# A new hand-recorded issue order for TensorE in an attention and gated feed-forward kernel, with a corrected planner's clock

## The chip, the cores and the metric

The kernel runs on one core of a Trainium2 chip. The metric is the time of one execution on the device, in microseconds (us). TensorE does matrix products (a 128 x 128 array of rows and columns); VectorE, ScalarE and GpSimd work element by element; SyncE (SP) issues nearly all DMA transfers. Results of products land in PSUM, which has eight banks of 128 x 512 fp32.

## The reference

What is computed, cut to what matters. There are 2048 tokens of 512 features, 32 heads of 16, and a hidden layer of 1792.

```python
x = A_x
xn = layernorm(x)                                    # over the 512 features, eps 1e-5
q, k, v = split_heads(xn @ A_wqkv)                   # 32 heads of 16
p = softmax(einsum("bhqd,bhkd->bhqk", q, k) * 16 ** -0.5)
s = merge_heads(einsum("bhqk,bhkd->bhqd", p, v)) @ A_wo
h = silu(xn @ B_w1) * (xn @ B_w3)
g = silu(h @ B_w2)
return x + s * g
```

All of it is fp32. Most products are made with numbers split in a high and a low part, three products instead of one (`split3`, `three`).

## The kernel before, in words

A prologue of some 160 us normalises x, transposes it, makes q, k and v and stores them. Then one long stretch does attention and feed-forward at the same time, and a tail does the projection with `wo` and the final sum.

**Attention** goes in 32 phases (16 pairs of heads, two halves of 1024 queries each). Three kinds of TensorE work belong to it:

- *Maxima* (letter m or M): `max_unit` multiplies 128 queries with 512 keys of one head; VectorE takes the row maximum out of the bank (line 391). When a phase's 64 maxima are there, `max_rows` reduces them, ScalarE negates them, TensorE turns them (line 404, the steps called by r and R), and four small DMAs write them as two extra rows of the queries, so that the score product subtracts the maximum by itself.
- *Scores* (s or S): `scores` multiplies 128 keys with 512 queries of one head (line 626); ScalarE takes the exponential out of the bank into one of 23 buffers `pt` (line 629, `PTS`).
- *Values* (v or r): `values` multiplies four buffers of exponentials with the values, four products side by side in 32 columns each (line 639), and adds up in the bank `pv`. One such group of four is a value block; 16 blocks make a phase, 512 the whole. After a phase, `take_out` copies `pv` out and, in several steps some us apart (`LATER`, `SOON`), fetches the row sums, makes their reciprocal, spreads it by DMA through HBM into `rb`, multiplies on GpSimd and stores the result.

**Feed-forward** (f or F): `gate` makes the hidden layer and the gate in four blocks of 512 tokens (`ORDER` 3, 0, 1, 2). `Lanes.emit` (line 857) issues each product in two halves of 64 rows.

Maxima, scores and gate products use 64 of the array's 128 rows each. A small letter uses the lower half (lane 0), a capital the upper half (lane 1), so that two of them run side by side. Value blocks and output tiles (o: `projecting`, with line 195, 197 and 199 in `split3`; `finish` at lines 1034 and 1035) use all 128 rows.

TensorE takes its instructions in program order. That order is written out by hand in the string `ORDER_OF_ISSUE`, one letter a product: the loop at the end goes through it, and puts off a letter (`late`) whose conditions aren't met. The conditions come from the class `Model`, the kernel's own account of time at build time: `half`, `whole`, `block` move TensorE's two lanes on, `work` moves the other engines on, and `free_at`, `ready`, `made` and `there` say when a bank, a phase, a hidden tile or a transfer is there by that account. The same account decides when the side work is issued: weight loads and splits (`Weights`), output steps (`small`, the list `outs`), final loads (`tend`). On the chip only semaphores count; the account only fixes the order. Seven banks go round by `take`; `pv` has the eighth.

An instruction waits for semaphores of other engines, and of its own engine where a buffer is written again; a second wait is an instruction of its own (`EVENT_SEMAPHORE`).

Of the kernel before, what the change touches and what calls it, by code (L numbers as in the profile page):

```python
# [41 lines left out]

LATER = (16.0, 1.5, 9.0, 16.0, 5.0, 0.0)
# [7 lines left out]
    "MfMfMfMffSSfSffMffMfMfSfSfMfsFFfFfFsMffMFfsMmFfFsFFfFmmFFfMmvvSffMMfMffMfSfMfFfFfFsFmFsFfFfFsFmFsFfF"  # L51
    "fMfSfMfSffMsFFfmFmFsFFfmFmFsFfFmFMffFmSvvsMsMfMvfSfMMmsFfFFffFSfFfsMfFFsMfsFFfMsfFfFFmMmvSfSmFfFmmFf"
    "FSfmFSfFffSFfmSFfmFSfFfFsmMfFMmvvSmmMfFFfFsfFfFFfsFMffFMfsFfFfMMsfFfFMmvSmSmfFFfFfSfMffFsMsFfFMfSfFf"
    "mFSfmFmFmFFfmSvvsMSmmSvSmMmsFrsMsMFfFfMfSfFfMmvSmmFFfSffMFfsFMffSFfsFFmFffMfSfSfFmFsFmFsFFfsFmFsFFsm"
    "FfFMfMfMfvvMmSsfMfSvvsMSsfFmFfFFfFmfSFsmFfFsFmFSfFfMfFfMfMmSfvsMMfMsvSfMmsFFsFfFfsFmFsFFfSmFfmFSffFm"
    "FmSvmSSsMffMvsMfMfMmSvSfMsMmvsSsFmFmFFffFsFFfMsfFsFMffSfFmFmFSfSfMfvsMSfSmfMvSmmSrsFmSmSvmSSffMfSfFF"
    "fmFsFsFMffSFfMfsFFfmSfFfFsSsFMmvvMsMssMvMsfMfSFsFfFfmSFfFmsFMfFfSfmFFfSfMfFsMfFfsFSfmMvMsSfmMfSvvSmM"
    "fSsSfvfMfSSfSsvMfsMsFfFsFFfFmsFfFFmSfMfSfFfmFSfFfMfsSfFmFSffFmFSffFmFsFFmmFFmvsSMfMffMSfvsMsMsMvsMMs"
    "MfvSmmMvSfMfSffMfSFfMfsFMfFfsMfFsFMfFfsFMfsFMffFsFmFfFsFmFFmsFfFmFsFfFMfFfMmvSmmSMfvSsMmvrSmmSmSvsMM"
    "mFmmFvvFmFsmFSfFffSMffFSfMfsFFsMfFfsFmFFsfFsMfFSfMfFfsFMffSfSMfFffSmFsFFfSmvSmmMSmvvSmfFFffSmFfSSfFm"  # L60
    "FfFsmFFsfFmFsFmFFssFFfmFFsFfmFsFFmfSfSvmSSfMmvsMfMSfFsfFFfMsFfFssFMffFsMfFmFfFsFmFMmvvsMmSSmvvSfMfSs"
    "SfvrsMMssSvmFsFSffMsFFfmFFsfFMsFfSfMfSffFmSfFFmFmMfvSmSfmMvSfMffSfMfFsFmFFsFfmFSfmFFfsFfMfSmFfFFmMfM"
    "mvvmMSssFmFvSmsSMsvsMFfSffMsFfFsMFffMfMSffFsFMffFSfmFFmFmvsMmFmSvSmMffSfFfSfFmSfFsFSfmFfFsFmFfSFffFm"
    "MMfFmvvSfMsMsfFfFFfsFSfMffFFsfSMfFfsFsFMfFfmMvsMmFmFsFvsMMsSsvMsfFfSmFfSFfMfsFSfMfSfFfmFSffFsMfFmFmF"
    "mFvvSmmSmFrSfFmFfSfmFMfsFMffFsFFmfFSffMfFSmFffFSsvMsMssFFmvsMmMsSvvmSfFfFfMSfFfmSfSfFfMsFfFmSfFFsFmf"
    "MfFsMvvSmsMsMvsMfMMfFsfFFfSfMffFSffMFmfSFfmFmFsFfFmFmFvSfSmmFfFFfFsfMfMFsfFsFfMFsFffMsFsFfMMffFmSvmS"
    "mMsFsFvSmMmmSvSsmMvSfMfFsfMfFSffMMfsFFfsFfMFsfFFmSffMFsFmvsMmSvSmFfSfmFfSfFmFfSFfmFsFfFmSfFSfmFFsfFR"
    "vmSfMMsSfvSmsSSmvMsSffFMfSfFfsMfFFfmSFfFsMfsFfFMsFffMsFsFFfmMvsMmSSmvvmSSffSMffMvvSffMMmMffSvSmSsfFf"
    "FFfFsFsFmfFFmFfFsmFfSFmFfsFFmFmSfFffFSfMffSMfsFFfMffSfMFfsMvvsMsMfMvSmMsfMvSmMffSSfFffFMffMsFFfMfsFf"
    "FsFfMsFfFMsfFsFfMsFfFfMsFsFFfMfsFfSfFmFfFSmsFvvsSmSmMvvSmmSmSvvSmFffFmFFfSfMfFffMmFSffFfFfMmFSfFmfFr"  # L70
    "sFfMmFMffFsFfFfFFfMmsFsFfMFfvvMffSfSMfSffSmFfFFfmSFfFmsFFfsFmFFfsFmFsFmFsFFfFsmFFssFsFvmSSmSmvvSmsFs"
    "FsFmFvmSmSfFFfSffFMfSfSfFmFffMSfFfFmFsSfmMvvMsmFFsmFFsvsMsFsMsFvMsFffSMffFSfMfSffSMffFFsmFfFMfmSvSmS"
    "mSsvmFsSsMvMsmFmSsFvsMfSfMfFfSfFMsFffMsFfFfSmFfFfSFmmFfMRvsMmSvSsmFmFmMvvMfMssFFfFfSfMfSfFfSfMfMffFs"
    "FFsFmFfFfMfMffSfSfMfSfFfFmFsFmFsFfFmSfFsFmFfFFmSmvvsMsSmMvSfMsSfFfFmFfsFmFfSFfmFsFsFSfmFfFmFfMvSmMmM"
    "svvsMSffSSmvMsfMfSfMfSfSffSFmFffSFmfFsFmFsFfFSmfFFmfFmFmMsvvSmFfFmsSFffFmSfFFfmFsFFfMsmFFfmFfSrsMMsf"
    "MvsMMfsMMfvSfMmSmvsMmFsFFfSffFsFMfsFFfmSfFMfSffMFfsFmFFfMmvsSmMfMvvMssMfMFfFfFfFssFFfMfFsfFFsMffMSff"
    "FfSFmFffSfMfSFfmFFsfFmFsFmFFsFfFsmFFmmSvvSmMsmSvsMSsMfSfvmSfSSmfSvmSMfMsvsMfMsFFfsFFfMsFfsFFmSffFsFM"
    "fSfmFmFfFMfSffMvSfMsfMsFfFFfMfsFMffFsMfFSfFfmFSfmFmFmFFfMsvvsMmSmSvSmsSfFFmFfFfmSFfSfmFfFsFmFFfsFmFf"
    "SSfMfRvMsmMsSvmSMmfMSfvsMfMMsvfSfMfSfMSffMSffMvvMfSfSmmFFfFfFsFfFsFmfFFsFmfSfSFmFfFsMfsFfFsMFfMfsFSf"
    "fFMfSffFmSFfMfmFSfvsSmMMsvvSmmFmSmFvSmsFsSvMsfFsFfMfFsFMsfFfMfFSffMFfsMfFfSsFMffFfMsFFsFfMffSFfMsfFM"  # L80
    "fsFFmFfMmvSsMsmFvmMsSMmvvSmmSmSvvSmsMmSvrSmFmfFFmsFfFSfFmFfSffMSfMfFfsFMfsFfFMfsFfFfMMsfFFfFsmFFmFfF"
    "fMffSSsvmSMfsMvvMsSmfFFffFsFmFFsFfmFsFFmfSFsfFmFFsfFmFsFfFMsFmFfSfMfFfmSvvsMmSSmvSmSffSmFFffFmFsFmFm"
    "FFsFfSffFFmSffMMfMfFfSsvvMsMsMmvvSfMfsFfSfFfFMfsMSfFfsFfFmFsFFfsFMffFSsmFvmSfSSfmFFffFfSmFfSfSfMfFFs"
    "sFmFfFsFMfFfmFmMvvsMmSmFrSmSmvSmSffSmFfFfFmSfFsFFmsFfFMsfFfFmFSffMMsvsMsMsMvsMMfMfSmvvMffSfSFffMfFfS"
    "fMFsSffMfFFsmFsFfFmFsFFmmFvvSmFfFfFmmSFffFSmfFFmSffFFsFmFsFfMffMSfMfvsMMmMsvsMmSvsFMsfFfMSfFfSfmFSff"
    "FSmfFFsmFFffSmSFfFmmFvSmMssMvsMMsMfvsMMsvsMfMMffSfFFfsFfFfMMsFfFfSfFmmFsFfFfFFmmSvSmfSFmFfSffFMsfFFs"
    "sFMfFfsFmFFffSmFfFSmrmSMfmSSfvSmMssMvsMsFfMsFFffFmSfFSfmFSfFfSmfFsFmFmFfFmSvSmmMSsvvMfMffMsSvvsFFmFs"
    "sFFsFmFfSfmFFffSMfSfFfMsfFfMFffMMfsMvsSmSmFvmSSssMvMsMsFsvMsfSfFmFSffFmSFffSMfFfSffMsFMfFfsFmFFffMfM"
    "fSfFFfmFsFFmsFFsFfFfmFFfFfMmmSvvsMSsSmvrSmSfSfMsvmSfMsFsFfFFfFsMfFfFsFfMsFsfMFfFfFfMfSffMMsvSsMsMmvv"
    "SfMffSfSfSfMfMmMvvMfSffMSfMffSfMfFfFsFmFmFsFfFfFsMsFfFmFsFfMfSfFfSmSfFfSmFfFmFsFfSfFmFmFfSsvvSmmSmSv"  # L90
    "vsFmFFmmFmFsFmFFsvSmMfFsFfsFFfMffSFmFfSfMffMfSFfSffMfSfFSffMfSfFMsfFmFsFmFvvSmsSsMvMsMfMsvsSMfFmfFfF"
    "sFFmsFfMfFMfsFfFSfFmfFsFMfFfSmfFFsfMfFSfMfSfmFsFFfSfmFSffFMmvvsMSmrsFmFFmmFsFsFFmvsSmFmFmMvvsMsFsFfM"
    "fFfFsFFmSfFmSfFffSmFfSfFmFfSmFvmSmSfSfSvvsMMffSfSFffFMsFfFsMfsFFfsMfFsFMfFsFfMmvsMmFfMFmvvSmfSFfFmfF"
    "FsmFFsfFMsFffSmFSffFMmfFFfMfMsvSmSmMfvSmMmvsMfFFsmFSfFfsFMffSSfmFFfFsfMSffFMsfFFfmFmMvvSfMfFsFfsFMff"
    "SFfSmFfSfmFSfFfmFsFFmSffFFfMfSffSfSRvsMfFFsFmFsfFmFsFsFmFFfFmFffMfMsMvsMfMSsvMsSmFsvmSmMSsvvMsfFSffS"
    "mFFffSmFfFSfmFfFSfmSFffMFfsFFfMffSfSmFfFFmsFFmFfsFmFFsfMFfSfMfFmFffSMsvvsMMsMsvsFMssMvsMMmSsvSmmMsFs"
    "FvsMSmSmvSmfFMfSffMfFSffMfFsFfSMffFFsFmFfFsmMvsMfMfMfSfFFffSFfmFmSFfFfmSfFmFmFSfmFfFmFvvSmMmfSFffFfF"
    "mFsFfFFffFsFMffFSfmFFmSfSfRvsMMssFvmSSssMvMsMssFvMsMssMvvMffSSfMffSfFmFSffFMsFfFsmFfSfFmSfFmFFmvvSms"
# [1242 lines left out]
```

## Time and profile before

| | |
|---|---|
| median of 3 runs | 1749.22 us (1748.68 to 1750.35) |
| profiled execution, first to last instruction | 1747.2 us |
| TensorE matmuls | 1737.2 us busy, 13188 |
| TensorE weight loads | 1027.4 us, 13188 |
| VectorE | 1432.9 us, 2343 |
| ScalarE | 1258.9 us, 2440 |
| GpSimd | 764.1 us, 791 |
| moved by DMA | 155.37 MB, 89 GB/s on average |

The times are those of the device; the span of the profiled execution leaves out what lies before the first and after the last instruction. Matmuls are pipelined, so a row of the timeline with `x8` may overlap the next one, and busy time of TensorE is more than the time in which it takes in operands: for distances, read the starts. In the profile, PE is TensorE's matmuls, PEld its weight loads, DVE VectorE, ACT ScalarE, POOL GpSimd, SP SyncE; L639 is line 639 of the kernel before. Tiles have the program's names: `e` a bank of scores, `m` of maxima, `f` of feed-forward, `o` of the output, `pt` exponentials, `mp` row maxima.

### The profile page before, as it was taken

Reading aid. Unit: us, or ns where it says so; the run is one execution under the profiler, and the core shown is the slowest. Engines: PE = TensorE matmul, PEld = TensorE weight load, DVE = VectorE, ACT = ScalarE, POOL = GpSimd, SP = SyncE. Lnnn points to the kernel's source line nnn. Section 1 sums busy time; section 2 is a strip of 40 time slices with the busy share of each in tenths; the row PEclk is TensorE's granted clock in tenths of the full one; section 3 lists DMA queues with packets and bytes.
Section 4 is the critical chain, followed back from the end, with each engine's and each line's share of the span. In section 5 each row is a group of like instructions: output and inputs, shape, how many; then the busy total and the mean of one; then the engine's idle time right before and its main releaser. Section 6 shows DMA issues by size and latency. Waiting matters only on the chain.

```text
span 1747.2 us, 35524 instructions
## 1 busy us (share of the span) xinstructions
PE 1737.2 (99%) x13188; PEld 1027.4 (59%) x13188; DVE 1432.9 (82%) x2343; ACT 1258.9 (72%) x2440; POOL 764.1 (44%) x791
## 2 busy tenths in 40 slices
PE   9999999999999999999999999999999999999998
PEld 7876655555555555555555565565555565555455
DVE  7576988888888888898888888898888897898625
ACT  4223788778878787778778877788787867868861
POOL 3102744346526561546356452555265615562101
PEclk9999999999999999999999999999999999999999
DMA  8657213132323222231433231132322321331542
GB/s 286 239 200 206 59 41 71 47 71 54 80 76 85 65 56 50 62 81 47 93 98 68 51 80 29 50 68 75 101 80 62 81 39 55 101 93 31 172 155 97
DMA packets 146798, 155.37 MB, mean 89 GB/s; under 512 B 42304, under 2 KB 100672, under 8 KB 143648
## 3 DMA queue, kind: packets, MB, share of 16 engines
q1 hardware_dynamic: 145760, 151.52, 32.0%
q8 instruction: 104, 1.70, 0.4%
q10 hardware_dynamic: 864, 1.57, 0.2%
q14 instruction: 70, 0.57, 0.1%
HBM read 107.97 MB, written 44.02 MB: 87 GB/s over the span
## 4 chain that ended last, share of the span: by engine, by line
PE 92%; issue 4%; DMA 2%; SPq 1%; DVE 0%; ACT 0%; POOL 0%; ACTq 0%; POOLq 0%
PE f L857 27%; PE pv L639 26%; PE e L626 17%; PE m L389 14%; PE m L507 2%; PE e L195 2%; PE e L199 2%; PE e L197 2%; PE m L480 0%; PE m L404 0%; DMA ovl<-o 0%; DMA wl<-g 0%; SPq L894 0%; DMA inh<-in_A_x_dram 0%; DMA last<-in_A_wo_dram 0%
## 5 line engine op out<-in xcount | busy, mean ns | idle before, releaser
L391 DVE TENSOR_REDUCE mp<-m 128x1 f32<-128x512 f32 x2048 | 1301.3, 684 | 192.2 <-PE m L389 123.8
L629 ACT ACTIVATE pt<-e 128x512 f32<-128x512 f32 x2048 | 1091.3, 605 | 301.9 <-PE m L389 130.7
L626 PE MATMUL e<-qs,ks 64*128 64x512 f32 x2048 | 713.2, 413 | 1.8 <-DMA qs<-ml 1.8
L389 PE MATMUL m<-ks,qs 62*128 62x512 f32 x2048 | 691.9, 411 | 0.2 <-DVE mp L391 0.2
L639 PE MATMUL pv<-pt,vt 128*17 128x512 f32 x4096 | 515.0, 597 | 0.0
L626 PEld LDWEIGHTS e<-qs,ks 64*128 64x128 f32 x2048 | 340.1, 184 | 266.8 <-ACT pt L629 87.9
L389 PEld LDWEIGHTS m<-ks,qs 62*128 62x128 f32 x2048 | 337.1, 184 | 123.3 <-ACT pt L629 39.6
L639 PEld LDWEIGHTS pv<-pt,vt 128*17 128x17 f32 x4096 | 81.1, 96 | 202.6 <-issue 194.3
L857 PE MATMUL f<-xtl,wh 64*128 64x512 f32 x488 | 171.8, 391 | 0.0
L857 PE MATMUL f<-xth,wl 64*128 64x512 f32 x488 | 171.7, 396 | 0.0
L857 PE MATMUL f<-xth,wh 64*128 64x512 f32 x488 | 169.0, 392 | 0.0
L742 POOL TENSOR_TENSOR h<-g,h 128x512 f32<-128x512 f32 x56 | 71.9, 1284 | 215.9 <-ACT h L738 215.8
L857 PE MATMUL f<-wh,hs 64*128 64x512 f32 x496 | 148.4, 395 | 0.0
L857 PE MATMUL f<-xth,xel 64*128 64x512 f32 x408 | 147.4, 396 | 0.0
L857 PE MATMUL f<-xth,xeh 64*128 64x512 f32 x408 | 144.7, 393 | 0.0
L857 PE MATMUL f<-xtl,xeh 64*128 64x512 f32 x408 | 143.9, 392 | 0.0
L322 POOL TENSOR_TENSOR wl<-wr,wh 128x512 fp32r<-128x512 f32 x92 | 118.4, 1287 | 7.7
L857 PE MATMUL f<-xeh,hs 64*128 64x512 f32 x400 | 121.5, 393 | 0.0
L321 POOL TENSOR_SCALAR wh<-wr 128x512 fp32r<-128x512 f32 x92 | 56.9, 619 | 115.1 <-PE m L389 47.7
L322 POOL TENSOR_TENSOR xel<-wr,xeh 128x512 fp32r<-128x512 f32 x76 | 97.9, 1288 | 6.3
L726 POOL TENSOR_SCALAR th<-th 128x512 f32<-128x512 f32 x56 | 34.6, 618 | 133.2 <-ACT th L719 133.2
L857 PEld LDWEIGHTS f<-xtl,wh 64*128 64x128 f32 x488 | 85.9, 185 | 6.8
(179 smaller groups left out, 2027.4 us busy)
## 6 DMA issues: line engine op xcount, KB each, us to landing
wr<-in_B_w_dram SPq DMA_DIRECT2D x168, 256.0 KB
qs<-qk SPq DMA_DIRECT2D x186, 64.0 KB
ks<-qk SPq DMA_DIRECT2D x90, 128.0 KB
qk<-sh SPq DMA_DIRECT2D x32, 256.0 KB
qk<-sl SPq DMA_DIRECT2D x32, 256.0 KB
v<-vrow SPq DMA_DIRECT2D x16, 272.0 KB
xin<-in_A_x_dram SPq DMA_DIRECT2D x16, 256.0 KB
g<-part SPq DMA_DIRECT2D x16, 256.0 KB
```

The costliest lines, as they stand in the source:

```text
L195: nc.tensor.matmul(ps, lhs[1], rhs[0], start=first, stop=False)
L197: nc.tensor.matmul(ps, lhs[0], rhs[1], start=False, stop=False)
L199: nc.tensor.matmul(ps, lhs[0], rhs[0], start=False, stop=last)
L321: nc.gpsimd.tensor_scalar(hi, t, 1.0, 1.0, op0=ALU.mult, op1=ALU.mult)
L322: nc.gpsimd.tensor_sub(lo, t, raw(hi))
L389: nc.tensor.matmul(ps, qs[p % 2][64 * h:64 * h + KM, q0:q0 + P], ks[p % 2][64 * h:64 * h + KM, c * 512:(c + 1) * 512], start=True, stop=True)
L391: nc.vector.reduce_max(mp[p, half][:, h, qt, c:c + 1], ps, axis=AX.X)
L626: nc.tensor.matmul(ps, ks[p % 2][64 * h:64 * h + KR, k * P:(k + 1) * P], qs[p % 2][64 * h:64 * h + KR, q0:q0 + 512], start=True, stop=True)
L629: nc.scalar.activation(pt, ps, AF.Exp, scale=DH ** -0.5)
L639: nc.tensor.matmul(pv[32 * j:32 * j + VW, :], vt[2 * p // GH][:, key, 2 * p % GH + j % 2, :], pt, start=key < 2 if last else k == 0, stop= ...
L742: nc.gpsimd.tensor_mul(h2, g, h2)
L857: nc.tensor.matmul(ps, left[r], right[r], start=starts and lane == 0, stop=ends and lane == 1)
```

## The change

1. The table `ORDER_OF_ISSUE` is another one: 8617 letters instead of 8614, with the same products of each kind. Value blocks stand in 259 runs instead of 381: 85 of one block, 113 of two, 35 of three, 16 of four, 9 of five and one of six, where there were 245 of one, 132 of two, three of three and one of four (r and R counted with them).
2. The account of time has other constants, a function `flip` for the turned row of maxima, a `done` that keeps results in the order of issue, and 4.3 us from the turned row to an open phase.
3. A second phase's output steps beyond the first two wait until the first phase's are done, and the account has GpSimd's 3.2 us for them.
4. Every twelfth exponential waits for the one three before it on its own engine, as a dependency added by hand (`add_manual_dep`). What later exponentials need of their own engine is known from that wait, so that they carry none.

The table is cut here to its first and last lines:

```diff
 ORDER_OF_ISSUE = (
-    "MfMfMfMffSSfSffMffMfMfSfSfMfsFFfFfFsMffMFfsMmFfFsFFfFmmFFfMmvvSffMMfMffMfSfMfFfFfFsFmFsFfFfFsFmFsFfF"
-    "fMfSfMfSffMsFFfmFmFsFFfmFmFsFfFmFMffFmSvvsMsMfMvfSfMMmsFfFFffFSfFfsMfFFsMfsFFfMsfFfFFmMmvSfSmFfFmmFf"
...
-    "vvsMmSmSvSmmSSmvSmmSSmSvsMSssMovSmsMSmoSmSssSvvMsSssMvMsMsMsvsMSsvMssSSsvMsSsvsMmMMvS......oSsSsSsSr"
-    "SoSsSsSssvvsSsSsSvovsSSssSSvSoSsSsSsvvoSsSsSvoSsSsSvvvvoSsSsSsovsSSsSsoSsSssSoSssSSsvvvovvoooSssSovo"
-    "SsSssSooovSsov"
+    "MffSMfSffSMfMfSffSMffSffMfsMfsMffSfsFFmFFsfMsfFmFsFFmFfSmFfFmfMFfmMvvsMSmfFFffFsMfFsFfmSFfsFmFFsfMsF"
+    "mFFffMMffMMfmMvvvMssSmFfFfFfMFsFfmSfFsFmFsFfMsfFFmSfFMffMSffsMvMsMffSfFfSFmSfFfMsfFSmFfSfFmFsFmFsFfF"
...
+    "sMvmSSmmSvSmFsmSoMssFFssMvMssFsMoSsSsSvvsMFsMsMFFSMSsFsFMSvSssSSsvvMsSMMFSsFMsSvSssSSsvvMSMFMSsMFsFM"
+    "SSMSvvvRoosFSsFssFSoSssSSsvvSsSssSoSsSsSsovsSSssSovvSssSSsvvvsSSsSsSoSssSSsovvSsSssSSvvvsSsSsSoSsSSS"
+    "Soovvvoooooooovvo"
 )
```

```diff
+AGO = mybir.DependencyInfo(mybir.DependencyClass.Sync, mybir.DependencyReason.DATA)
...
-        SLOT, LOAD, TURN, VALUES, CLEAR, LATENCY, NOTICE = 0.232, 0.1, 0.097, 0.858, 0.983, 0.44, 0.054
-        COST = {"act": 0.495, "dve": 0.605}
-        DONE = {"act": 0.107, "dve": 0.078}
+        SLOT, LOAD, TURN, VALUES, CLEAR, LATENCY, NOTICE, FLIP = 0.232, 0.1, 0.097, 0.858, 0.983, 0.448, 0.054, 0.11
+        COST = {"act": 0.488, "dve": 0.602}
+        DONE = {"act": 0.112, "dve": 0.081}
...
             self.turned = False
-            return begins
+            self.done = max(self.done, begins)
+            return self.done
...
+        def flip(self, there):
+
+            begins = max(max(self.lane) + self.TURN, there + self.LOAD, self.issue)
+            self.issue = max(self.issue, there)
+            self.lane, self.begun = [begins + self.FLIP] * 2, [begins] * 2
+            self.done = max(self.done, begins)
+            self.clear = begins + self.FLIP + self.CLEAR - self.VALUES
+            self.turned = False
+            return begins
...
-        begins = mod.whole(0.1, was_free[i] + mod.NOTICE)
+        begins = mod.flip(was_free[i] + mod.NOTICE)
...
-        free_at[i] = mod.work("dve", mod.work("act", begins + 0.5, 0.25), 0.28)
+        free_at[i] = mod.work("dve", mod.work("act", begins + 0.32, 0.25), 0.28)
+        landed[p * 2 + half] = free_at[i] + 4.3
...
-        nc.scalar.activation(pt, ps, AF.Exp, scale=DH ** -0.5)
+        done = nc.scalar.activation(pt, ps, AF.Exp, scale=DH ** -0.5)
+        recent.append(done.ins)
+        if len(recent) % 12 == 0:
+            tc.add_manual_dep(done.ins, recent[-4].name, AGO)
...
-                    mod.work("act", lanes.begins + mod.LATENCY, 0.6)
+                    mod.work("act", lanes.begins + mod.LATENCY, 0.5)
...
-                ready[c[3]] = mod.free["dve"] + 3.5
+                ready[c[3]] = landed[c[3]]
...
-            if c[0] <= mod.now and not any(r[2] for r in rows):
+            if c[0] <= mod.now and not any(r[2] for r in rows) and (c is outs[0] or c[3] < 2):
                 c[3] += 1
+                if c[3] == 4:
+                    mod.work("pool", mod.now, 3.2)
                 c[0] = mod.now + (LATER if c[2] < PHASES - 4 else SOON)[c[3]]
```

More of the change, by code (lines that the diff above doesn't have):

```diff
@@ new lines @@
+    "mSvvSmfSfMSffFfMSffMfSfFmFsFMffSsFFfmFFffMSffMfsFFFmsFsFFfmsFfFMsfFFmSfmFFfMffSMmvvmSMsMsvMmFsSmsFvm"
+    "SMmMmvvRFsmFFsFmFsFsmFFffSfMfSfMfSfFFmfSffMSffMMsvmMMssSvmSFmsFfFSfFmfSFfMsFfFsMsFFfmSFffMsfFMFffMfS"
+    "sMvSmMmFsFsvsMFmFsSmvSmmMmSvvmSmSmSvSmFsfMfSfFfMfSfMfSFfMfsFMffSsFFfmFFffMfSfMfsFFFmsfFFsFmFsFfMsFFf"
+    "mSFfFmfMMffMsvvMmMmMmvvvMsfSfMfFSfFmSfFfSfMfFsFmfFFsfMFsMfFsFffMSfFmFfSffMSmvMssSMmvmSsSfMrSfMffSMff"
+    "SfMfSfsFFmFsFfMsFFfmsFFMfsFsfFMfFsFmFsFmFsFfMfFsFFmsFFfMfMffSmSvmSSmMmvvSmMmsSvMffMMmmSvvfSfMfSfMSff"
@@ new lines @@
+    "MfSfSFfmFsFFfmFsFFmsFFmFfsFFmFfsFmFsFmfFSfFsFmFFfMfSfffMSMffSffMfSsMvvvvvFmFsFmsFFsmFsFFmFmFsFsFmFFf"
+    "sFFfsfMfSFfMfSfMfFsFmFfFffMSfSffMfSMffMSffMSffMrvSmsMmMvvSmMsSmvsMFmFsFfsFfMFsFfmSFfsFmFsFFfmSFfFmsF"
+    "sFfFmFsFfMfSFfmFFffMfSfMfSfSffMFsFfmFsFmFsFfFmFsFFmfFmFMfmMvvvmSSsmMvmSSmfSfMvSmmMsMvvmSfMfSfSfFFmfS"
+    "FmFsFmFfSfMfFsFfSfMFsFfmFFffMfSfMfSffSfMFsfMfFsFmsFFfFmSfFmFsFsFfmFmFMmvvvmSSsmSvvRMsfSFfMfSfFmFsfFf"
+    "SMsFFfmFsFfMsFffSMfSFfmFFffMSfffMSFfsfMsFfFmFsFmFsFFmFfsFmFSffMfFmMvvvMsfMfSFsFffMFsFfmSFfsFmFFsfMFs"
@@ new lines @@
+    "FfmSFfFmffMSfmMvvmSmSMsvvSmSsmMvmFFsFmFssFmFfFfSfMfSfMfSfFMfsfFMfSffSFmFFffMffMsFFfMfFsFfsFMFsFfmSFf"
+    "FmsFfFmFfMfMmMvvvSmMsmMvvmSFmFsFfsFfMFsFfmSfFFsmFsFfMfSfFmSfFfMfSfMfSsvvvRsMfSFfMfsFFmFsfFFsMfSfFmfS"
+    "fFMsfFfMSffSFmFFffMSffmFFsFmFsFsfFMFfsFmfSfFMsfFmFFffSMMsvvmSSssSvvSmSmSmvvMsmMmSvvMfSffMSfMffSfsFFm"
+    "FFsfMsfFmFsFFmfFSmfFfFFfMfSfMfSfSffMsFFfmsFFmFsFFfmFsFFmsFFfMfMfMfmSvvMssMMmvvmSMfsFFffSfMfSfMfSfFmF"
+    "sFMffSfFFsmFFsfMsFfMfSfmFFffSfMMmvvmSmSsMvvRSfMfSfMfSffMfSfSffMFsFfmSfFFmsFFsFfmFFsfMFsfFFmsFmFfSFfs"
@@ L138 @@
+    "sMvmSSmmSvSmFsmSoMssFFssMvMssFsMoSsSsSvvsMFsMsMFFSMSsFsFMSvSssSSsvvMsSMMFSsFMsSvSssSSsvvsMSMFMSsMFsF"
+    "MSSMSvvvRoosFSsFssFSoSssSSsvvSsSssSoSsSsSsovsSSssSovvSssSSsvvvsSSsSsSoSssSSsovvSsSssSSvvvsSsSsSoSsSS"
+    "Soovvvoooooooovvo"
 )
@@ L242, in start @@
             self.lane, self.begun = [0.0, 0.0], [0.0, 0.0]
-            self.issue = self.clear = 0.0
+            self.issue = self.clear = self.done = 0.0
             self.free = {"act": 0.0, "dve": 0.0, "pool": 0.0, "dma": 0.0}
@@ L273, in whole @@
             self.turned = True
+            self.done = max(self.done, begins + took - self.SLOT)
+            return begins
[6 more added lines that the diff above has]
+            self.turned = False
             return begins
```

153 lines of the change are left out of this document (70 added, 83 removed).

## The prediction

> **What bounds the kernel now.** I read the busy shares first, then TensorE's own waits, then the order of time around a few value blocks.
>
> ```profile
> PE 1737.2 (99%) x13188; PEld 1027.4 (59%) x13188; DVE 1432.9 (82%) x2343; ACT 1258.9 (72%) x2440; POOL 764.1 (44%) x791
> PE 92%; issue 4%; DMA 2%; SPq 1%; DVE 0%; ACT 0%; POOL 0%; ACTq 0%; POOLq 0%
> 160.70:1621.80 1461.10, 1459.05 (x11753) 840.10 (x11752) 1267.21 (x2060) 1145.98 (x2213) 719.41 (x735) 1.00 0.28 68
> PE e L626 <- DMA qs<-ml: 1.8, 1, 1.8
> PE m L389 <- DVE mp L391: 0.2, 1, 0.2
> ```
>
> The rows are the busy shares, the chain of waits, the stretch from the first to the last gate product (columns PE, PEld, DVE, ACT, POOL, clock, DMA), and all that PE waited for in that stretch. TensorE is the bound: it hardly ever waits, at full clock (1.00). But busy is not work: matmuls overlap, so I look at starts. The timeline, with its columns start, length, engine, line:
>
> ```profile
> 800.15 0.40 PE L389 MATMUL m<-ks,qs 62*128 62x512 f32 x1
> 800.48 1.05 PE L639 MATMUL pv<-pt,vt 128*17 128x512 f32 x8
> 801.46 0.50 PE L626 MATMUL e<-qs,ks 64*128 64x512 f32 x1
> 802.03 1.89 DVE L391 TENSOR_REDUCE mp<-m 128x1 f32<-128x512 f32 x3 [0.27 <-PE m L389]
> 802.36 1.91 PE L639 MATMUL pv<-pt,vt 128*17 128x512 f32 x16
> 804.20 0.49 PE L389 MATMUL m<-ks,qs 62*128 62x512 f32 x1
> 804.53 0.39 PE L389 MATMUL m<-ks,qs 62*128 62x512 f32 x1
> 804.73 1.89 DVE L391 TENSOR_REDUCE mp<-m 128x1 f32<-128x512 f32 x3 [0.81 <-PE f L857]
> 1683.34 0.40 PE L197 MATMUL o<-wh,ovh 128*128 128x512 f32 x1
> 1685.66 0.40 PE L199 MATMUL o<-ks,ovh 128*128 128x512 f32 x1
> ```
>
> A product's slot: the last two rows lie ten output products apart, 2.32 us, so 0.232 us each. Two half products (scores, maxima, gate), one on each half of the rows, share such a slot. A change of mode costs three times over. Going in: 800.15 to 800.48 is 0.33, 0.10 over a slot. The block: alone it takes 800.48 to 801.46, 0.98 us; two take 802.36 to 804.20, 1.84 us; so a block more costs 0.86 and the first one 0.12 over that. Coming out: 804.20 to 804.53 is again 0.33, 0.10 over. Together **0.32 us for each stretch of half products**, however long.
>
> Does that account for the time? The counts of products in the same stretch of the page:
>
> ```profile
> L626 PE MATMUL e<-qs,ks 64*128 64x512 f32 x2048 | 713.2, 413 | 1.8 <-DMA qs<-ml 1.8
> L389 PE MATMUL m<-ks,qs 62*128 62x512 f32 x1984 | 680.2, 410 | 0.2 <-DVE mp L391 0.2
> L639 PE MATMUL pv<-pt,vt 128*17 128x512 f32 x4096 | 515.0, 597 | 0.0
> L404 PE MATMUL m<-ident,nm 128*16 128x128 f32 x31 | 8.6, 277 | 0.5 <-ACT pt L629 0.5
> 160.70:1747.20 1586.50, 60.01 (x264) 44.90 (x264) 20.11 (x33) 1.00 0.29 74
> ```
>
> The last row is the output products (tile o) alone. With the 4032 gate products that the table lists, halves: (2048+1984+4032)/2 x 0.232 = 935; value blocks (4096/8 = 512) x 0.86 = 440; outputs 264 x 0.232 = 61; turned rows 31 x about 0.2 = 6; changes of mode: the old table has 385 stretches of half products, x 0.32 = 123; the last store about 6. That is 1571 of 1586.5 us. So about **15 us is all that waiting for other engines can cost now**; the table replays nearly as planned. What is left to gain is the 123 us.
>
> **The change part by part.**
>
> *Fewer changes of mode.* I counted both tables. All products are the same in number (4032 f/F, 2048 s/S, 1984 m/M, 512 blocks, 22 o). Runs of value blocks: 381 before, 259 after. With runs of output tiles, half products are cut into 385 stretches before and 264 after: 121 x 0.32 = **-38.7 us**. Nothing covers these: they are TensorE's own time.
>
> *Uneven halves.* A stretch lasts as long as its longer half. Summed over the stretches, the longer half has 4044 products before and 4081 after (364 of 385 stretches were even, now 196 of 264): 37 x 0.232 = **+8.6 us**.
>
> *Several products running on one half.* Three or more in a row on one half occur 0 times before and in some 60 places after. No row of before shows what that costs. If the other half's next weights have to queue behind the third one's, that half starts late by the 0.10 us that the first product after a change costs (804.53 above). It matters only where that half isn't two ahead already, in 29 places: an estimate of **+3 us**, between 0 and the 15.8 of the first rival.
>
> *Waiting for exponentials.* A longer run needs up to 20 of the 23 exponential buffers full at once. Counting the PE work that the table puts between a block's last score product and the block: median 4.6 us before, 5.8 after; below 1.6 us in 27 blocks before, 18 after. So value blocks wait less, not more. Taken 0; bounds -4 (the rest above shared out) and +4.
>
> *Maxima.* VectorE's cover is thinner. Three maxima back to back take 1.89 us at 0.684 for one, so 0.60 each. I come back to it in the rivals; taken +2.
>
> *ScalarE's own waits.*
>
> ```profile
> L629 ACTq EVENT_SEMAPHORE  x576: 17/17/17, 164.5 to 1723.5; - x192
> 807.77 4.03 ACT L629 ACTIVATE pt<-e 128x512 f32<-128x512 f32 x8 [1.18 <-PE e L626]
> ```
>
> 576 extra wait instructions of 17 ns go down to some 170: at most 7 us of an engine that is busy 72%; and exponentials run 0.49 us apart ((4.03-0.6)/7) with those waits among them. The added wait, each twelfth exponential on the one three before, is for one begun 3 x 0.49 = 1.47 us earlier and 0.6 long: done before it is asked for. Behind it stand the later exponentials and copies, for which banks and value blocks wait; none is held. If ScalarE became the bound, the 7 us would be the gain. **0**, between -2 and +1.
>
> *Output steps kept apart.* A second output's reciprocal, store (rd), four loads (rb), three GpSimd products and eight stores now stand behind the first one's. One output's waits add up to 47.5 us in the plan and phases follow each other every 1461/30 = 48.7 us, so two seldom overlap by more than their first step, which is still let through. **0**; if they did, eight stores at 0.42 us on SP would be late, 3 us that nothing but the outputs at the end waits for.
>
> *Account of time and rows of maxima.* The constants only decide what the plan does. A phase now opens 4.3 us after its row was turned: worth the one wait of PE for DMA above, 1.8 us at most. Taken -1.
>
> *The tail.* The last gate product comes after block 494 instead of 476, so 18 blocks of bare tail are left instead of 36.
>
> ```profile
> L857 PE MATMUL f<-wh,hs x496: 383/392/501, 270.2 to 1621.6; 64*128 64x512 f32 x166
> 1621.80:1747.20 125.40, 118.98 (x706) 64.61 (x703) 60.57 (x96) 67.52 (x136) 12.63 (x12) 1.00 0.42 139
> 1635.28 5.55 DMA wl<-g
> ```
>
> The tail's PE was not idle before, so nothing is won there but changes of mode, counted already. Now the gate of the last block must be stored and fetched back before its first output tile: that took from 1621.6, the last start in the first row, to 1635.28 + 5.55 = 1640.8 in the third, 19 us. The new table leaves some 40 half products (4.6), 8 blocks (6.9), two tiles (5.6), two small ones (1.4) and nine changes (2.9) in between: 21 us. It just fits. Taken +1, bounds 0 and +8.
>
> **The sum**: -38.7 + 8.6 + 3 + 2 - 1 + 1 = -25. The profiled execution spans 1747.2 us, 2.0 under the runs' median; on the median that makes **1724 us**.
>
> **The rivals.**
>
> *Strict order of starts.* The upper half can't begin a product before one issued earlier on the lower half has begun. Then each product that runs ahead by more than one costs a slot: I count 68 such slots in 46 stretches after and none before, 68 x 0.232 = 15.8 instead of 3, so **1737 us**. Against it:
>
> ```profile
> 1606.39 0.39 PE L857 MATMUL f<-xeh,hs 64*128 64x512 f32 x1
> 1606.49 0.40 PE L626 MATMUL e<-qs,ks 64*128 64x512 f32 x1
> 1606.63 0.39 PE L389 MATMUL m<-ks,qs 62*128 62x512 f32 x1
> 1606.86 0.39 PE L857 MATMUL f<-xel,hs 64*128 64x512 f32 x1
> ```
>
> The table has "m S F f" here: m is issued before S, yet S begins at 1606.49 and m at 1606.63. The halves are 0.13 apart and stay so. But a tenth of a microsecond is not a slot, so a chance is left. The Trainium skill, "TensorE: Matmul & The Clock Gate", in the section on packing small matmuls, says that matmuls start and end strictly in program order; by that rule it would be the 1737. These rows disagree with it.
>
> *VectorE can't keep up (ends slower).*
>
> ```profile
> L391 DVE TENSOR_REDUCE mp<-m 128x1 f32<-128x512 f32 x2048 | 1301.3, 684 | 192.2 <-PE m L389 123.8
> ```
>
> The row of the maxima: VectorE idles 192 us ahead of them in all. In the brackets further up it idled 0.27 us ahead of one stretch and 0.81 around a pair of blocks, so I put 0.27 on a run's first block, 0.54 on its second, and on each later one, with no maxima left in the banks, all of its 0.86. Old table: 381 x 0.27 + 136 x 0.54 + 5 x 0.86 = 181, so between the value runs it has next to nothing to spare. New: 259 x 0.27 + 174 x 0.54 + 98 x 0.86 = 248. There are 192 - 25 for the shorter span + 12 because maxima end some four blocks later: 179. It lacks 69 us. Against: gate products need nothing of VectorE, and the new table keeps some until its last maxima, so TensorE has other work while VectorE catches up, and is held only where a maximum product stands at the head of its queue without a bank. The case decides once TensorE is held for 25 us. With half of the 69: 1724 + 35 = **1759 us**.
>
> *Gain given back in the tail.* Loads and stores of the last gate block come late, S and output tiles alone remain, and ScalarE's 62 exponentials at 0.49 (30 us) set the pace where PE wants its tiles: 10 to 15 us lost, **1734 to 1739**.
>
> *The change does not do what it says*: products that find no free bank in the plan are put off, and runs split again. Half of the 121 changes back is 19 us, less half of the uneven halves, 4: **1739**.
>
> **How the numbers follow.** Forecast (1714 to 1734): 0.62. Strict starts 0.08, tail 0.11, runs split 0.04, all faster still. VectorE 0.11, of which 0.08 slower and 0.03 near no change. Others about no change 0.04. A measurement tells about 0.2%, 3.5 us, from no change. So faster 0.85, same 0.07, slower 0.08. The range runs from 1711 (no cost of uneven loads, all waits of PE gone) to 1743, which leaves out VectorE's case and half of what lies about no change.
>
> **What would show it.** Right: a value run still takes 0.98 us for its first block and 0.86 for each other; PE's waits stay under 5 us; ScalarE's wait instructions at the exponentials are near 170; VectorE's idle ahead of maxima falls from 192 towards 170. Wrong: gaps of over 0.33 us ahead of value runs or inside half stretches; score or maximum products waiting for VectorE; in the stretches with "fff" between upper products, an upper half idle for 0.23 us; in the tail, output tiles waiting for the stored gate.

## The result, and the profile after

| | before | after |
|---|---|---|
| median on the device | 1748.95 us (1748.62 to 1750.35) | 1720.12 us (1719.59 to 1721.86) |
| ratio, 95% interval | | 0.9835 (0.9821 to 0.9849) |
| profiled execution, first to last instruction | 1747.2 us | 1717.8 us |

The change is 28.8 us faster, where 25 were forecast. One of the eleven executions of t6 below took 3330 us and is left out of its figures. First the busy shares of the kernel after, then its row of the maxima, its stretch from the first to the last gate product, and all that TensorE's matmuls waited for between 160.7 and 1690 us. After the change L403 is the product of the maxima, L405 their reduction, L643 the scores, L646 the exponential, L659 the values, L877 the gate.

```profile
PE 1708.2 (99%) x13188; PEld 1102.6 (64%) x13188; DVE 1408.0 (82%) x2343; ACT 1224.0 (71%) x2440; POOL 765.5 (45%) x791
L405 DVE TENSOR_REDUCE mp<-m 128x1 f32<-128x512 f32 x2048 | 1276.8, 684 | 174.6 <-PE m L403 103.6
```

```profile
160.70:1635.10 1474.40, 1471.85 (x12020) 931.31 (x12021) 1264.84 (x2098) 1142.27 (x2275) 722.65 (x737) 1.00 0.28 69
```

```profile
PE e L643 <- DMA qs<-ml: 2.5, 1, 2.5
```

The picture is that of before: TensorE busy 99%, clock 1.00, one wait of 2.5 us in the whole stretch. The engine that was to be overtaxed, VectorE, has the same 82%, and idles 174.6 us ahead of maxima where it idled 192.2.

The timeline of the kernel after, around two runs of two blocks:

```profile
822.44 0.42 PE L403 MATMUL m<-ks,qs 62*128 62x512 f32 x1
822.44 0.39 PE L877 MATMUL f<-xeh,hs 64*128 64x512 f32 x1
822.79 1.91 PE L659 MATMUL pv<-pt,vt 128*17 128x512 f32 x16
824.63 0.50 PE L643 MATMUL e<-qs,ks 64*128 64x512 f32 x1
824.64 0.73 PE L403 MATMUL m<-ks,qs 62*128 62x512 f32 x2
824.98 0.39 PE L643 MATMUL e<-qs,ks 64*128 64x512 f32 x1
825.21 0.40 PE L403 MATMUL m<-ks,qs 62*128 62x512 f32 x2
825.54 1.91 PE L659 MATMUL pv<-pt,vt 128*17 128x512 f32 x16
827.38 0.50 PE L643 MATMUL e<-qs,ks 64*128 64x512 f32 x1
```

A change of mode costs about what it did: 822.44 to 822.79 is 0.35 going in, 822.79 to 824.63 is 1.84 for two blocks, 824.63 to 824.98 is 0.35 coming out. These two steps are 0.02 longer than those shown of before, but over the whole traces the median step in is 0.325 us after and 0.323 before. There are only fewer of them.

Where the 28.8 us went can be read from the starts of TensorE's products alone, summed over both traces from the first gate product to the last output product (1580.4 us before, 1551.5 after). I cut that time into stretches of half products, runs of value blocks, and the rest:

| | before | after | difference |
|---|---|---|---|
| stretches of half products | 384 | 264 | -120 |
| value runs, output tiles, turned rows, and the steps into and out of them, beyond the slot of the last half product | 590.8 | 562.4 | -28.4 |
| first product of a stretch: 0.110 us each | 42.2 | 29.0 | -13.2 |
| slots of the longer half (4044 and 4081 by the letters, at 0.2315) | 936.2 | 944.8 | +8.6 |
| what is left inside the stretches | 11.2 | 15.3 | +4.1 |
| sum | 1580.4 | 1551.5 | -28.9 |

The 0.110 is the part of a stretch's length beyond its slots that stays when no weight load in it is held (what that is stands at t11), by a fit over the stretches: 0.1105 before, 0.1102 after. What is left inside the stretches includes TensorE's few waits there, 2.0 us before and 2.5 after, so without them it is 9.2 and 12.8. The changes of mode are the rows of the value runs and of the first products together: -41.6. Of these, -36.7 are the plain value runs (338 before, 223 after, 0.319 us each), -1.8 the groups with a turned row (31 and 30), and -3.1 the groups with output tiles (15 and 11).

### The profile page after: what moved, and what is told of

Its sections match the earlier page's. It is cut to its first block, busy times and chain, and to the rows that moved or that the text cites. A ratio compares the mean times of both kernels' runs of the same rounds, so it can differ in the third digit from the quotient of the medians.

```text
span 1717.8 us, 35102 instructions
## 1 busy us (share of the span) xinstructions
PE 1708.2 (99%) x13188; PEld 1102.6 (64%) x13188; DVE 1408.0 (82%) x2343; ACT 1224.0 (71%) x2440; POOL 765.5 (45%) x791
## 4 chain that ended last, share of the span: by engine, by line
PE 95%; issue 2%; DMA 2%; SPq 1%; DVE 0%; ACT 0%; POOL 0%; ACTq 0%; POOLq 0%; DVEq 0%
PE f L877 28%; PE pv L659 27%; PE m L403 17%; PE e L643 15%; PE m L522 2%; PE e L197 2%; PE e L201 2%; PE e L199 2%; PE m L495 0%; PE m L418 0%; DMA ovl<-o 0%; SPq L695 0%; DMA wr<-in_A_wqkv_dram 0%; DMA ovh<-o 0%; DMA inh<-in_A_x_dram 0%
## 5 line engine op out<-in xcount | busy, mean ns | idle before, releaser
L405 DVE TENSOR_REDUCE mp<-m 128x1 f32<-128x512 f32 x2048 | 1276.8, 684 | 174.6 <-PE m L403 103.6
L646 ACT ACTIVATE pt<-e 128x512 f32<-128x512 f32 x2048 | 1061.0, 612 | 260.7 <-PE e L643 139.1
L643 PE MATMUL e<-qs,ks 64*128 64x512 f32 x2048 | 726.4, 408 | 2.5 <-DMA qs<-ml 2.5
L403 PE MATMUL m<-ks,qs 62*128 62x512 f32 x2048 | 725.6, 415 | 0.0
L659 PE MATMUL pv<-pt,vt 128*17 128x512 f32 x4096 | 489.8, 595 | 0.0
L403 PEld LDWEIGHTS m<-ks,qs 62*128 62x128 f32 x2048 | 339.1, 184 | 146.9 <-ACT pt L646 34.6
L643 PEld LDWEIGHTS e<-qs,ks 64*128 64x128 f32 x2048 | 345.1, 184 | 120.5 <-issue 35.0
L659 PEld LDWEIGHTS pv<-pt,vt 128*17 128x17 f32 x4096 | 94.2, 96 | 235.9 <-issue 229.1
L877 PE MATMUL f<-xtl,wh 64*128 64x512 f32 x488 | 177.9, 391 | 0.0
L877 PE MATMUL f<-xth,wl 64*128 64x512 f32 x488 | 176.1, 393 | 0.0
L877 PE MATMUL f<-xth,wh 64*128 64x512 f32 x488 | 174.4, 391 | 0.0
L877 PE MATMUL f<-wh,hs 64*128 64x512 f32 x496 | 157.8, 393 | 0.0
L877 PE MATMUL f<-xtl,xeh 64*128 64x512 f32 x408 | 148.7, 391 | 0.0
L877 PE MATMUL f<-xth,xel 64*128 64x512 f32 x408 | 143.4, 394 | 0.0
L877 PE MATMUL f<-xth,xeh 64*128 64x512 f32 x408 | 142.6, 392 | 0.0
L877 PE MATMUL f<-xeh,hs 64*128 64x512 f32 x400 | 127.1, 392 | 0.0
L796 POOL TENSOR_SCALAR th<-th 128x512 f32<-128x512 f32 x16 | 9.9, 619 | 187.5 <-ACT th L792 187.5
L877 PE MATMUL f<-wl,hs 64*128 64x512 f32 x248 | 92.3, 392 | 0.0
```

Source lines behind the costliest of these rows:

```text
L403: nc.tensor.matmul(ps, qs[p % 2][64 * h:64 * h + KM, q0:q0 + P], ks[p % 2][64 * h:64 * h + KM, c * 512:(c + 1) * 512], start=True, stop=True)
L405: nc.vector.reduce_max(mp[p, half][:, h, qt, c:c + 1], ps, axis=AX.X)
L643: nc.tensor.matmul(ps, ks[p % 2][64 * h:64 * h + KR, k * P:(k + 1) * P], qs[p % 2][64 * h:64 * h + KR, q0:q0 + 512], start=True, stop=True)
L646: done = nc.scalar.activation(pt, ps, AF.Exp, scale=DH ** -0.5)
L659: nc.tensor.matmul(pv[32 * j:32 * j + VW, :], vt[2 * p // GH][:, key, 2 * p % GH + j % 2, :], pt, start=key < 2 if last else k == 0, stop= ...
L877: nc.tensor.matmul(ps, left[r], right[r], start=starts and lane == 0, stop=ends and lane == 1)
```

## The experiments

**The table alone, and everything but the table.** t1 is the kernel before with the new `ORDER_OF_ISSUE`, t2 the changed kernel with the old one.

```diff
 ORDER_OF_ISSUE = (
-    (old table)
+    (new table)          # t1, in the kernel before; the reverse for t2, in the kernel after
 )
```

> The kernel before with the new table alone: the old account of time, the old output steps, all of ScalarE's own waits. Runs theory (the time goes with the changes of TensorE's mode): all of the gain, 1718 to 1724 us. Rival (the mended account and the fewer waits are needed for the table to hold): 1730 to 1745, with gaps ahead of value runs.

> The changed kernel with the old table: new account, outputs kept apart, few own waits of ScalarE. Runs theory: nothing is gained without the table, 1745 to 1756 us (the new account puts off some 20 letters of a table that was made for the old one). Rival (the waits and the account carry a part): 1735 to 1742.

t1 took 1725.07 us, ratio 0.9862 (0.9848 to 0.9875), a microsecond outside the 1718 to 1724 and far from the rival's 1730. t2 took 1751.91, ratio 1.0012 (1.0003 to 1.0021). So the table by itself brings 24.8 us, and the rest without it costs 2. A likely reason is that the corrected account doesn't fit the old table, whose replay then puts off 20 half products where it put off three; no run shows it. With the new table the rest brings another 4 to 5 us. The next two runs ask which part of it does.

**ScalarE's own waits, and the output steps.** t3 takes the added dependency out of the changed kernel, t4 lets output steps overlap again.

```diff
-        if len(recent) % 12 == 0:
-            tc.add_manual_dep(done.ins, recent[-4].name, AGO)                   # t3
...
-            if c[0] <= mod.now and not any(r[2] for r in rows) and (c is outs[0] or c[3] < 2):
+            if c[0] <= mod.now and not any(r[2] for r in rows):                 # t4
...
-                if c[3] == 4:
-                    mod.work("pool", mod.now, 3.2)                              # t4
```

> The changed kernel without the added dependency, so that ScalarE's own waits are back (about 576 wait instructions at the exponentials). Runs theory: the same as the changed kernel within 0.2%, 1717 to 1723 us. Rival (own waits delay the exponentials that longer value runs wait for): 1724 to 1732.

> The changed kernel with the output steps as before: a second phase's may run along with the first's, and the account has no GpSimd time for them. Runs theory: no change, 1717 to 1723 us. Rival (output steps collide on GpSimd and in the buffer of reciprocals and hold the gate's splits up): 1724 to 1735, with TensorE waiting for GpSimd.

t3 took 1724.05, ratio 0.9855 (0.9842 to 0.9869); t4 took 1720.77, ratio 0.9836 (0.9823 to 0.985). The output steps are worth nothing, as forecast. The own waits are worth 3 to 4 us: the two intervals overlap, but t3's four executions (1722.83 to 1725.55) all lie above t4's (1720.58 to 1721.04) and the kernel after's (1719.59 to 1721.86). That is the rival of t3, at its lower end. ScalarE's wait instructions at the exponentials, in the kernel after and in t3:

```profile
L646 ACTq EVENT_SEMAPHORE  x110: 17/17/17, 164.5 to 1669.5; - x110
```

```profile
L646 ACTq EVENT_SEMAPHORE  x628: 17/17/17, 164.2 to 1669.4; - x157
```

The two traces hold the same table, so their 264 stretches can be set side by side: t3's take 2.55 us longer in all, of which 1.79 fall to the 65 stretches of over 60 products, and the steps into value runs 0.96 longer. That is the 3.5 us between the two. Elsewhere nothing differs.

**The same part by itself in the kernel before (t10).**

```diff
-        nc.scalar.activation(pt, ps, AF.Exp, scale=DH ** -0.5)
+        done = nc.scalar.activation(pt, ps, AF.Exp, scale=DH ** -0.5)
+        recent.append(done.ins)
+        if len(recent) % 12 == 0:
+            tc.add_manual_dep(done.ins, recent[-4].name, AGO)
```

> The kernel before with one part of the change alone: every twelfth exponential waits for the one three before it on its own engine. Table, account and output steps as before. Theory formed after t1 and t3 (an exponential that finds ScalarE idle starts about 0.06 us later when it carries a wait on its own engine, its bank comes free later, and TensorE's half products wait for it): 2 to 4 us faster than 1749.9, so 1746 to 1748. Rival (the prediction: only ScalarE's occupancy counts, and that is hidden): 1749 to 1751, no difference.

It took 1749.6, ratio 0.9997 (0.9988 to 1.0006): no gain. The wait instructions fell here too, from the 576 shown above:

```profile
L632 ACTq EVENT_SEMAPHORE  x103: 17/17/17, 164.7 to 1712.6; - x103
```

So what I expected of t10 was wrong: the own waits cost nothing with the old table. In both tables exponentials start 0.02 us sooner after their score product without them (mean in stretches of 40 products and more: 0.583 to 0.563 in the old table, 0.587 to 0.563 in the new one). Only in the new table does TensorE come out ahead for it. Two differences of the tables could be the reason. The new one has 65 stretches of over 60 products, the old one 31, and 1.79 of the 2.55 us are in those. And in the new one more weight loads stand waiting for ScalarE with no time to spare (the counts are at t11). That either is the reason is argued and not shown.

**The price of a change of mode (t5).** The changed kernel with 57 runs of value blocks split: the next two half products go between their blocks.

```diff
-    ... "MFfmMvvsMSmf" ...
+    ... "MFfmMvsMvSmf" ...       # at 57 runs
```

> The changed kernel with 57 of its runs of value blocks split: the first two half products behind the run stand inside it instead, so that there are 321 stretches of half products instead of 264 and not one product more. Runs theory: 57 x 0.32 = 18 us more, 1736 to 1741 us. Rival (what long runs cost in idle VectorE and ScalarE time balances their saving, so that splitting costs less): under 1732.

It took 1738.8, ratio 0.9938 (0.9924 to 0.9952): 18.7 us more than the kernel after by the medians, 17.9 by the starts in the traces, so 0.31 to 0.33 for each split. The 0.32 read off three pairs of starts holds. The traces have 120 stretches fewer after the change, where my -38.7 counted 121, so at this price they make 38 to 39 of the -41.6. What goes beyond lies at the turned rows and the output tiles. Six turned rows stood inside a run of value blocks before and cut it in two (387 runs in the trace, 381 in the letters), at 0.55 us each beyond blocks and slots where the others cost 0.45; after, none does. And four groups with output tiles fewer brought 3.1 us, where 0.32 each makes 1.3. No run tested these two.

**Several products on one half (t6, t7).** The kernel before with 60 places rearranged, where two or three products in a row go to one half and then as many to the other; each is the same product as before.

```diff
-    ... "MMfMffMfSfMfFf" ...
+    ... "MMfMfffMSfMfFf" ...       # t6: "fMfS" becomes "ffMS" and the like
...
-    ... "MMfMffMfSfMfFf" ...
+    ... "MMfMffffMSMfFf" ...       # t7: "fMfSfM" becomes "fffMSM" and the like
```

> The kernel before with the order inside 60 of its stretches of half products changed at one place: two products of the lower half in a row, then two of the upper (llUU for lUlU). Strict order of starts: the upper half is a slot late from there on, 60 x 0.232 = 14 us more, 1763. Weights in order: about 0.1 us each, 6 us, 1756. Free halves: no change, 1748 to 1752.

> The same with three in a row (lllUUU for lUlUlU) at 60 places. Strict order of starts: two slots, 60 x 0.464 = 28 us more, 1778. Weights in order: the upper half's weights stand behind the third lower ones, which wait for the second to begin, 0.33 us each, 20 us, 1770. Free halves: no change beyond 4 us.

t6 took 1752.91, ratio 1.0018 (1.0009 to 1.0027), t7 took 1760.0, ratio 1.006 (1.0047 to 1.0074): 3.0 and 10.1 us for 60 places. Per changed stretch the median is 0.02 us for two ahead and 0.17 for three. A strict order of starts would have cost a slot of 0.23 for each place of t6, 14 us, and two for each of t7, 28. It is refuted. The 10.1 us of t7 are also neither the 20 of weights in order nor the 4 at most of free halves; what the 0.17 consists of stays open. The Trainium skill, "TensorE: Matmul & The Clock Gate", in its section on packing small matmuls, has starts and ends strictly in program order; with 3.0 and 10.1 instead of 14 and 28 these runs do not agree with it for products on different halves of the rows.

**The same in the changed kernel, the other way round (t9).** 54 of its 82 stretches in which one half runs two or more ahead are put in an order where it doesn't.

```diff
-    ... "FmFfSmFFfmfMFfm" ...
+    ... "FmFfSmFfFmfMFfm" ...
```

> The changed kernel with the order inside 58 stretches of half products rearranged, so that no half runs more than one product ahead of the other where the counts allow it: 54 of the 82 stretches with two or more extra products in a row on one half lose them. Same products in each stretch, 264 stretches, 259 runs of value blocks, 4081 slots; the planner puts nothing off, and its table ends 0.6 us later. Theory (running three ahead costs about 0.17 us a stretch, two ahead 0.02, as t6 and t7 measured): these stretches are mostly two ahead and some three, so 2 to 5 us faster than the changed kernel's 1720.5, 1716 to 1719. Rival 1 (the prediction's third term was too large, such starts cost nothing): 1720 to 1722. Rival 2 (strict order of starts): 12 to 13 us faster, 1708.

It took 1722.05, ratio 0.9841 (0.9827 to 0.9854), beside 0.9835 (0.9821 to 0.9849) of the changed kernel: nothing gained, where 2 to 5 us were expected. After t6 and t7 I had held that running ahead made the +4.1 us inside the stretches. That theory falls: what is left inside the stretches must in the main have another cause.

**Does VectorE run short (t8)?** The changed kernel with a small extra reduction (8 columns of a spare tile) on VectorE after every fourth maximum.

```diff
         nc.vector.reduce_max(mp[p, half][:, h, qt, c:c + 1], ps, axis=AX.X)
+        tick[0] += 1
+        if tick[0] % 4 == 0:
+            nc.vector.reduce_max(spare[:, 8:9], spare[:, 0:8], axis=AX.X)
```

> The changed kernel with one small reduction of 8 columns added on VectorE behind every fourth maximum, 512 in all, some 0.1 us each and so about 50 us more of its time. It adds nothing to the result. If VectorE has room (forecast): up to 5 us more. If it is as good as the bound (the rival that ends slower): 30 to 50 us more.

It took 1726.01, ratio 0.9865 (0.9852 to 0.9879). Its rows of VectorE, and what TensorE waited for:

```profile
L408 DVE TENSOR_REDUCE mp<-m 128x1 f32<-128x512 f32 x2048 | 1295.8, 683 | 157.6 <-PE m L406 101.1 <-PE e L649 44.9 <-PE f L883 6.0
L411 DVE TENSOR_REDUCE spare<-spare 128x1 f32<-128x8 f32 x512 | 77.3, 151 | 0.0
```

```profile
PE e L649 <- DMA qs<-ml: 2.5, 1, 2.5
```

The small reductions overlap with their neighbours: maxima follow each other 0.598 us apart, and 0.666 with a small one between them (medians over the trace), so the 77.3 us recorded are some 512 x 0.068 = 35 us of VectorE's turn. Of these, 5.9 came out at the end. If VectorE lacked time already, as the rival had it, all 35 would have. It is near its limit and not over it. The 5.9 us, a little over the 5 of the forecast, do not show among the waits of the matmuls, which name VectorE nowhere. They show by the starts: the part left inside the stretches is 20.7 us here and 15.3 in the kernel after.

**What holds the half products (t11, t12).** A weight load can wait for the engine that reads the bank its product will write, as the second row below does. In the traces many weight loads of half products start 0.05 us after the end of an instruction of the engine whose semaphore they wait for; I call these held. One of them in the kernel after, with the exponentials of the same moment, and below it two rows of a load that isn't held, with its product; the columns are those of the timeline, and the second exponential ends with the first row:

```profile
827.91 1.09 ACT L646 ACTIVATE pt<-e 128x512 f32<-128x512 f32 x2 [1.66 <-PE m L403]
828.56 0.18 PEld L403 LDWEIGHTS m<-ks,qs 62*128 62x128 f32 x1 [0.19 <-ACT pt L646]
828.56 0.50 PE L403 MATMUL m<-ks,qs 62*128 62x512 f32 x1
828.19 0.18 PEld L877 LDWEIGHTS f<-wh,hs 64*128 64x128 f32 x1
828.41 0.39 PE L877 MATMUL f<-wh,hs 64*128 64x512 f32 x1
```

The load at 828.56 was released by the first exponential, which began at 827.91 and lasts some 0.6 us. Its product starts with it, while the load at 828.19 is 0.22 ahead of its own. Counted over the traces (50 to 60 ns behind an end): 427 held by ScalarE and 636 by VectorE before, 732 and 999 after, 833 and 962 in t3. (The expectations below go by a count that leaves out part of ScalarE's: 411 and 632.) Leaving out the first stretch, a stretch of the kernel after with none of them outlasts its slots by 0.113, one with ten to nineteen by 0.213; but the first kind has 6 products on average and the second 64, so these figures don't tell a held load from mere length.

Most held loads cost nothing. A load that isn't held starts 0.23 us ahead of its product (median), a held one 0.20 before the change and 0.14 after. In the kernel after, products whose held load led by more than 0.02 us follow the one before on their half within 0.01 us of a slot (means); those whose load led by 0.02 us or less come 0.07 us late. Of the latter kind, with the first product of each half in a stretch left out:

| loads with no lead, held by | ScalarE | VectorE |
|---|---|---|
| before | 18 | 23 |
| t10 (before, few own waits) | 12 | 24 |
| t12 (before, short maxima) | 18 | 3 |
| after | 38 | 50 |
| t3 (after, own waits back) | 84 | 46 |
| t11 (after, short maxima) | 59 | 1 |

The new table has twice as many as the old one, and giving ScalarE its own waits back adds 46 there, where taking them away saves 6 in the old table. This goes with a gain in the one and none in the other. It is a count all the same: in t3 ScalarE's are late by 0.04 us on average instead of 0.07, so that it doesn't add up to the 2.55 us.

t11 and t12 are the kernels after and before with half of VectorE's reduction left out, so that it gives banks back sooner:

```diff
-        nc.vector.reduce_max(mp[p, half][:, h, qt, c:c + 1], ps, axis=AX.X)
+        nc.vector.reduce_max(mp[p, half][:, h, qt, c:c + 1], ps[:, 0:256], axis=AX.X)
...
-        ... nc.scalar.activation(pt, ps, AF.Exp, scale=DH ** -0.5)
+        ... nc.scalar.activation(pt, ps, AF.Exp, scale=0.125 * DH ** -0.5)
```

> The changed kernel with each row maximum taken over 256 of the 512 keys (half the reduction left out), and the exponential's factor an eighth so that it stays finite; TensorE's work and the order are untouched. VectorE gives banks back some 0.27 us sooner. Theory (half products are held by banks given back late: in the changed kernel 995 weight loads start 0.05 us after the end of a VectorE instruction and 632 after one of ScalarE, and the stretches that hold them are longer; a fit over the stretches puts 8.4 us on VectorE's and 3.8 on ScalarE's): 6 to 11 us faster than the changed kernel's 1720.5, 1710 to 1714, and few loads left that start 0.05 us behind VectorE. Rival (the extra length lies in the order of the two halves): 0 to 2 us faster, 1718.5 to 1721.

> The same edit in the kernel before. There 635 weight loads start 0.05 us behind VectorE and 411 behind ScalarE, and the fit puts 6.2 and 1.6 us on them. Theory (banks): 4 to 7 us faster than 1749.9, 1743 to 1746. Rival (order of the halves, and the old table has no uneven starts): 0 to 1 us faster, 1749 to 1750.

t11 took 1717.74, ratio 0.9817 (0.9803 to 0.983); t12 took 1747.55, ratio 0.9988 (0.9979 to 0.9997). The row of the maxima in t11:

```profile
L405 DVE TENSOR_REDUCE mp<-m 128x1 f32<-128x256 f32 x2048 | 816.9, 421 | 591.6 <-PE m L403 356.4
```

0.26 us less for each maximum (0.684 to 0.421), 592 us idle ahead of them, and hardly a load is held by VectorE any more (9, where it was 999). That brought 2.4 us in the changed kernel, and 2.84 in its stretches by the starts; in the kernel before it brought 2.2 by the medians, but 0.7 in its stretches by the starts. Both times lie between the two theories: banks given back late do lengthen the stretches, by a third or less of what I put on VectorE, and the loads then meet ScalarE instead (732 held by it become 799). Whether this explains why the new table has more left inside its stretches than the old one stays open: by the medians both gain alike, by the starts of one trace each the new table gains 2.1 us more, over half of the 3.6 (9.2 to 12.8). What remains inside the stretches of t11 beyond slots and first products is still 12.5 us, of which 2.5 are the wait for a phase's row. That part of the rest is ScalarE's side fits t3; no run took that side away.

## Why the prediction was right

The forecast was 1724 us; the run gave 1720.12, within the likeliest case. Term by term:

- **Fewer changes of mode.** Forecast -38.7, measured -41.6. Price and mechanism hold: 0.31 to 0.33 each by t5, 0.319 for the plain value runs, and the rows of a value run are unchanged. The count of stretches was right to one (120 in the traces). The 2.9 us beyond lie at the turned rows that no longer cut a run and at the output tiles, which I priced like all others.
- **Uneven halves.** Forecast +8.6. No run took it by itself, and the accounting of starts uses the same count of letters, so it doesn't confirm it. The trace speaks for less: among the kernel after's stretches of 60 products and more, the 32 even ones outlast the slots of their longer half by 0.303 us (median), the 30 uneven by one by 0.207. So there the odd product seems to cost some 0.14 of its 0.232, and what is left inside the stretches would be larger by as much as this term is smaller.
- **Several products on one half, and maxima.** Forecast +3 and +2; what is left inside the stretches rose by 4.1. The size was near and the first cause wrong: taking such an order away (t9) gained nothing. I had no row for running ahead and took the loading of the first product after a change for it. Part of what stands there instead is weight loads held until their product is due (t11 took 2.8 us away with VectorE's); the trace of before had 1063 held loads, 41 of them with no lead. I looked at the waits of the matmuls only, where they don't appear. The cause of the rest is open.
- **Waiting for exponentials.** Forecast 0. The step from a half product into a value run has a median of 0.325 us after and 0.323 before; one in twenty takes 0.39 or more, where it was 0.36. By the means that is some 1.5 us over 242 steps, within the bounds of 4.
- **ScalarE's own waits.** This is the step that failed. Forecast 0 between -2 and +1; with the new table it is about -3 (t3). I took ScalarE's busy share of 72% as proof that 17 ns more or less are hidden. That share doesn't say when a bank comes free. Of the exponentials in t3 that found ScalarE idle, the 141 with an own wait began at least 0.483 us after the start of their score product (5th percentile), the 172 without one 0.428; the kernel after has 29 and 277 of them. A twentieth of a microsecond on a bank whose next weight load has no lead can become TensorE's. That it does so by this way is argued; that the own waits cost 3 to 4 us with this table, and nothing with the old one, is what t3, t4 and t10 show. The number of wait instructions that I named as a sign (near 170) was off as well: 110.
- **Output steps, account, tail.** Forecast 0, -1, +1. Output steps: 0 by t4. The account with the output steps is the difference of t1 and t3, 1.0 us, as forecast, though within what these runs can tell; not for the reason given, since the wait for a phase's row, 1.8 us before, is 2.5 in t1, in t3 and in the kernel after. The tail: 21 us were forecast from the last gate product to the first output tile of that block.

```profile
L877 PE MATMUL f<-wh,hs x496: 383/391/501, 290.0 to 1635.1; 64*128 64x512 f32 x166
1656.25 0.50 PE L197 MATMUL o<-ks,ovl 128*128 128x512 f32 x1
```

The first row, from the view of the gate's line, ends with its last start at 1635.1; the second is that tile in the timeline: 21.15 us. TensorE's waits after 1620 us come to 0.3. The stored gate was there in time.

So -25 became -28.8 mostly by what turned rows and output tiles saved beyond the price (-2.9). The other two errors cancelled: without the saved own waits the +4.1 inside the stretches would be 6.7, and the steps into value runs 1 us longer, more than the 5 that I gave; the own waits, which I gave nothing, took that back. The mechanism that carries the forecast is right; that the small terms came out so near is luck.

**The rivals.** *Strict order of starts*: refuted by t6 and t7, and by t9, where it would have given 12 us. *VectorE can't keep up*: refuted by t8, and by a time 39 us below what it gave. My count had it 69 us short: 248 us idle at the value runs. Measured between 175 and 1600 us (counting VectorE as taken until the next maximum could start, and each stretch from 0.6 us after its first product to 0.6 after its last) it is 197, against 174 before, and inside the stretches of half products its idle time fell from 81 to 38. The slack that I had put at next to nothing between the value runs was there, and the new order uses it. *Tail*: refuted by the 0.3 us. *Runs split again*: the trace has 259 value runs, as the table.

**The signs.** First block 0.98 and others 0.86: seen. Waits under 5 us: 2.5. VectorE's idle towards 170: 174.6. Wait instructions near 170: no, 110.

## What to carry to other kernels

Where TensorE is busy all the time, price its changes of mode from the starts of its products and count them in the order of issue; here that sum held to 8%. A share of busy time does not tell whether an engine's delay is hidden: look at which weight loads start a few hundredths after that engine's instructions end, and above all at how many of these have no lead left before their product. And a small edit to another engine can be worth nothing with one order of work and 3 us with another, so test it in the kernel it will live in.

## What the runs showed of the hardware

- Products on different halves of the rows need not start in the order of issue: two ahead on one half cost 0.02 us (median of 60 places), three ahead 0.17.
- In the kernel after, products whose weight load starts 0.02 us or less before them, held by ScalarE or VectorE, come 0.07 us late on average; those whose held load had more lead are on time within 0.01.
- A change from half products to value blocks and back costs 0.31 to 0.33 us, however long the stretch between (57 more of them took 17.9 to 18.7 us).
- An exponential that finds ScalarE idle starts some 0.055 us later when it carries a wait on its own engine (0.483 against 0.428), three times the 17 ns of the wait instruction.
- A reduction of 8 columns is recorded with 0.151 us on VectorE, and moves the next maximum by 0.068.
